# Decode attention with a gated MLP on one core: one weight load cut into three by lanes and rows, and the input loaded in one transfer

## The chip, the cores and the metric

The kernel runs on one core of one Trainium2 chip. The metric is the device time of one execution in microseconds (us). Before the change it is 661.74 us, the median of three runs (661.59, 661.74, 661.86).

The core has a tensor engine (PE), a vector engine (DVE), a scalar engine (ACT), a general engine (POOL) and a synchronization engine (SP). Transfers are started from the queues of SP and ACT, and sixteen DMA engines, shared by both queues, move the bytes.

## The reference

The result is `x + A(layernorm(x)) + B(layernorm(x))` for 4 batch entries of one token with D = 640, all in bf16. A is attention over a cache of 4096 positions, 32 heads of 128; B is a small gated MLP. Cut to what matters:

```python
def _A_ref(x, k_cache, v_cache, wq, wo):      # caches: (4, 32, 4096, 128)
    q = (x @ wq).reshape(B, Sq, Hq, Dh).transpose(0, 2, 1, 3)
    scores = jnp.einsum('bhqd,bhkd->bhqk', q, k_cache) * Dh ** (-0.5)
    p = softmax(scores, axis=-1)
    o = jnp.einsum('bhqk,bhkd->bhqd', p, v_cache)
    return o.transpose(0, 2, 1, 3).reshape(B, Sq, Hq * Dh) @ wo      # wo: (4096, 640)

def _B_ref(x, w_in, w_sp, b_sp, w_out):       # w_in: (640, 1728), w_out: (864, 640)
    z = gelu(x @ w_in)
    g = w_sp * layernorm(z[..., Fh:]) + b_sp
    return (z[..., :Fh] * g) @ w_out

xn = layernorm(x)
return x + _A_ref(xn, ...) + _B_ref(xn, ...)
```

The two caches are 134 MB each, so nearly all of the 282 MB that the kernel reads are caches. Each is read once.

## The kernel before

**Units.** The 32 heads are cut into four groups of eight. A unit `u` is one group and one batch entry, so there are sixteen. For a unit the 8 heads × 4096 positions are spread over the 128 lanes (partitions) of the on-chip memory: each lane holds 256 positions of one head, 64 KB of K and 64 KB of V. A transfer of one unit's K or V is 8 MB, 64 KB a lane.

**Scores.** DVE multiplies K by the query (`product`, L539), adds the two halves of the head dimension (`fold_half`, L545), and PE sums the rest with an identity matrix (`sums`, L557). Four such steps make a unit. DVE then reduces to scores and maxima (L571 to L590), ACT takes the exponential (L598), DVE spreads it by head (L609), and PE weights V with it (`weighted`, L633).

**Groups.** After the four units of a group, `group_turn` (L674 to L693) divides by the denominators and transposes on DVE, and `group_proj` (L701) multiplies by the group's eight rows of output weights `wo_sb`, adding into `out_ps`. The last group is done with its own layout by head.

**Places.** K goes through a ring of seven slots of 16 KB a lane; V has one place, `v_all`, which holds `wq` and `w_in` before the first V. The output weights of a group lie in ring slot 4 (`WO_AT`), 10,240 bytes a lane: 8 rows of 640 bf16. Lane `p` gets rows `8p` to `8p + 7` of the group's weights, which lie side by side in memory.

**Order of loads.** All big loads are issued on SP's queue, in the order of the list `loads`. `pump()` issues the next one as soon as the code that frees its slots stands behind it in the program; on the chip SP then waits for the semaphores of the instructions that used the slot. For a group in the middle the order is V of unit u, K of unit u + 2, and after the group's fourth V and K the group's `wo` (L235 of `load_wo`), then the next V. The small x goes on ACT's queue at the very start (L103), three transfers of 2, 1 and 1 of its four rows, into ring slot 1.

**Semaphores.** The transfers of both queues share eight completion semaphores in turn, the x loads among them: a transfer first waits for the one that had its semaphore eight transfers earlier. The first x load has semaphore 0, `wq` 1, the other two x loads 2 and 3, the first two K loads 4 and 5, the two one-element loads of the MLP (L737, L738) 6 and 7; `w_in` comes next and waits for semaphore 0, `w_out` for 1, and so on.

**B's output weights.** The 864 rows of `w_out` are three parts: 5 rows on each of 128 lanes, 1 row on each of 128 lanes, and 8 rows on each of 12 lanes; the last is loaded by four transfers (L126) of three lanes each, 10,240 bytes a lane.

Of the kernel before, what the change touches and what calls it, by code (L numbers as in the profile page):

```python
# [17 lines left out]
def kernel(  # L18
# [14 lines left out]
    nc = tc.nc  # L33
    P = nc.NUM_PARTITIONS
# [31 lines left out]
    def up(n):  # L66
        return -(-n // 256) * 256

    PW = sum(up(r * D) for _, r, _ in W_OUT[1:])
    CUT = (0, 320, D)  # L70
    CB = 4
    NG = NR // CB
    GW = CB * Dh
    QH = QD // PAR
    JR = Dh // QH
# [18 lines left out]
    p_end = p_buf[:, 2 * NR * HT :]  # L94
    p_m = p_buf[:, 0 : 2 * NR * HT].rearrange("p (n g c h) -> p n g c h", n=2, g=NG, c=CB)

# [1 line left out]

    ring = places.tile([P, RING, QW], BF16, name="k_ring")
    x_bf = ring[0:Bsz, 1, 0:D]  # L100
    x_rows = A_x.flatten_outer_dims()
    for b0, b1 in ((0, 2), (2, 3), (3, 4)):
        nc.scalar.dma_start(out=x_bf[b0:b1], in_=x_rows[b0:b1])  # L103
    v_all = places.tile([P, NK * QW], BF16, name="v_all")

    wq_sb = v_all[:, 0 : DC * HD].rearrange("p (c n) -> p c n", c=DC)
# [87 lines left out]
    def wo_load(hg):  # L194
        return (lambda: load_wo(hg)), [WO_AT]
# [27 lines left out]
    wo_sb = ring[:, WO_AT, 0 : HT * D].rearrange("p (h n) -> p h n", n=D)  # L223

    def load_wo(hg):
        rows = A_wo[hg * HT * Dh : (hg + 1) * HT * Dh]
        if hg == HG - 1:
            by_head = rows.rearrange("(h p) n -> p h n", p=P)
            for h0, h1 in ((0, 2), (2, 4), (4, 6), (6, 7)):
                nc.sync.dma_start(out=wo_sb[:, h0:h1, :], in_=by_head[:, h0:h1, :])  # L230
            for half in range(2):
                cols = slice(CUT[half], CUT[half + 1])
                nc.sync.dma_start(out=wo_sb[:, HT - 1, cols], in_=by_head[:, HT - 1, cols])
            return
        nc.sync.dma_start(  # L235
            out=wo_sb, in_=rows.rearrange("(p j) n -> p j n", j=JR)
        )

    pump()

# [4 lines left out]
    for e in range(PAR):  # L245
        nc.gpsimd.tensor_copy(
            out=of_row[:, e, :, :, e, :],
            in_=ident[:].rearrange("p (k q) -> p q k", q=QD)[:, 0:Bsz, :, None].to_broadcast(
                [P, Bsz, NQ, LN]
            ),  # L250
# [18 lines left out]
    for i in range(NSTAT):  # L269
# [5 lines left out]
        out=rstd[:], in_=mv[:, 1:2], func=ACT.Sqrt, bias=eps_tile[:Bsz], scale=1.0  # L275
# [4 lines left out]
        out=xn_bf,  # L280
# [12 lines left out]
    for c in range(DC):  # L293
        nc.tensor.transpose(
            out=xnT_ps[:, c, :], in_=xn_v[:, c, :], identity=ident[:Bsz, :Bsz]
# [8 lines left out]
    for e in range(PAR):  # L304
        q_ps = ps_pv.tile([P, HG, Dh], FP32, tag="pv", name="q_ps")
        for c in range(DC):
            for k in range(NQ):
                nc.tensor.matmul(  # L308
                    out=q_ps[k * QD : (k + 1) * QD],
# [5 lines left out]
        rows = const.tile([P, HG, Dh], BF16, name=f"q_rows{e}")  # L315
        nc.vector.tensor_scalar(  # L316
            out=rows[:], in0=q_ps[:], scalar1=scale_qk, scalar2=None, op0=ALU.mult
# [4 lines left out]

    hot = const.tile([P, CB, HT], FP32)
    nc.vector.tensor_reduce(
        out=hot[:].rearrange("p c h -> p (c h)"),
        in_=ident[:].rearrange("p (g m) -> p m g", m=QD),
        axis=AX.X,
        op=ALU.add,
    )
    pick = const.tile([P, CB, P + Bsz - 1], FP32)  # L330
    nc.gpsimd.memset(pick[:], 0.0)
    nc.gpsimd.tensor_copy(
        out=pick[:, :, Bsz - 1 :].rearrange("p c (k q) -> p c k q", q=QD)[
            :, :, :, 0 : PAR * Bsz : Bsz
        ],
        in_=hot[:].rearrange("p c (k e) -> p c k e", e=PAR),
# [4 lines left out]
        out=of_set[:],  # L341
        in_=hot[:].rearrange("p c h -> p (c h)")[:, 0 : PAR * Bsz].rearrange(
            "p (e b) -> p e b", b=Bsz
        ),
# [5 lines left out]
    with nc.allow_low_precision("0 and 1"):  # L350
        nc.vector.tensor_reduce(
            out=own[:],
            in_=ident[:].rearrange("p (h l) -> p h l", h=HT),
# [5 lines left out]
        out=par[:], in_=own[:].rearrange("p (k e) -> p e k", e=PAR), axis=AX.X, op=ALU.add  # L359
# [3 lines left out]
        out=far[:],  # L363
# [6 lines left out]

    out_ps = ps_out.tile([P, max(CUT[1], D - CUT[1])], FP32)
    OG = 32

    def out_sum(half, rows=Bsz):
        return out_ps[OG * half : OG * half + rows, 0 : CUT[half + 1] - CUT[half]]

    for half in range(2):
        nc.tensor.matmul(  # L378
            out=out_sum(half, OG),
            lhsT=ident[:Bsz, :OG],  # L380
            rhs=x_bf[:, CUT[half] : CUT[half + 1]],
            start=True,
# [19 lines left out]
    def gmlp():  # L402
# [100 lines left out]
        for k, (w, _, n, _) in enumerate(w_rows):  # L503
            for half in range(2):
                nc.tensor.matmul(
                    out=out_sum(half),
                    lhsT=gm["yT"][0:n, k, :],
                    rhs=w[:, CUT[half] : CUT[half + 1]],
                    start=False,
# [97 lines left out]
    def by_head(u):  # L607
        hg, b = divmod(u, Bsz)
        nc.vector.tensor_tensor(  # L609
            out=p_m[:, u % 2],  # L610
            in0=p_c.pop(u)[:].rearrange("p (g c) -> p g c", c=CB)[:, :, :, None].to_broadcast(
                [P, NG, CB, HT]
# [85 lines left out]
    def group_proj(hg):  # L698
        for n, o in enumerate(gr.pop(hg)):
            for half in range(2):  # L700
                nc.tensor.matmul(  # L701
                    out=out_sum(half),
                    lhsT=o,
                    rhs=wo_sb[:, n, CUT[half] : CUT[half + 1]],
                    start=False,
# [29 lines left out]
    with tc.manual_schedule(engines={E.PE, E.DVE, E.Activation, E.SP}):  # L735
# [5 lines left out]
        for n in range(NK * NU):  # L741
# [55 lines left out]
            out=den[:],  # L797
# [12 lines left out]
        for c in range(NC):  # L810
            nc.tensor.matmul(  # L811
                out=o_last[0][:, :, :, b],
# [44 lines left out]
```

## Time and profile before

| | before |
|---|---|
| median of the runs | 661.74 us |
| the profiled execution's own time | 661.84 us |
| its span in the profile | 660.0 us |
| bytes read from HBM | 282.24 MB |
| mean rate over the span | 428 GB/s |
| PE busy | 313.5 us, 47% |
| DVE busy | 522.5 us, 79% |
| ACT busy | 29.9 us, 5% |
| POOL busy | 6.4 us, 1% |
| granted clock of PE, mean | 0.68 |
| `wo` loads of groups 0 to 2, issue to landing | 20.3 us, median |

The span runs from the first to the last instruction of the profiled execution; its own time is 1.84 us more. Besides busy times the profile has the chain of work that ended last, a timeline of each engine's instructions and of the DMA issues of each queue, and records of the DMA engines: of every packet its start, its duration and its size (not which engine moved it), and of every transfer the times at which the DMA engines raised its completion semaphore.

### The profile page before, as it was taken

The numbers are of one execution on the slowest core, as the hardware profiler recorded it, in microseconds if no ns is written. First come the engines' busy times: TensorE is split into PE (matmuls) and PEld (weight loads), VectorE is DVE, ScalarE is ACT, GpSimd is POOL, SyncE is SP. The second block draws the span as 40 slices with busy tenths as digits, with TensorE's granted clock in tenths as the row PEclk, the third lists the DMA queues.
The fourth block names the chain that finished last, engine by engine and source line by source line (L and its number), as shares of the span: only waits on it lengthen the run. The fifth ranks groups of instructions, "written<-read, shape, count | busy, mean of one in ns | idle before, by whom it ended". The sixth has DMA issues, their size and how long they took to land.

```text
span 660.0 us, 4780 instructions
## 1 busy us (share of the span) xinstructions
PE 313.5 (47%) x2083; PEld 134.3 (20%) x2083; DVE 522.5 (79%) x274; ACT 29.9 (5%) x73; POOL 6.4 (1%) x21
## 2 busy tenths in 40 slices
PE   0564362536426362462536436363462634637366
PEld 0231120212212121130212212121130211212124
DVE  1767978969597795969959598695969969999960
ACT  0020000000000000000000000000000000000000
POOL 2100000000000000000000000000000000000000
PEclk9665585766858677675865767667676866776566
DMA  9999999999999999999999999999999999999997
GB/s 372 434 454 441 413 441 438 425 441 442 421 441 434 433 434 433 433 418 437 442 441 437 410 441 441 434 429 429 434 441 433 434 417 449 413 435 434 449 408 289
DMA packets 8224, 282.55 MB, mean 428 GB/s; under 512 B 888, under 2 KB 2176, under 8 KB 2560
## 3 DMA queue, kind: packets, MB, share of 16 engines
q1 hardware_dynamic: 8184, 282.24, 99.1%
q8 instruction: 16, 0.26, 0.1%
q14 instruction: 4, 0.03, 0.0%
q10 hardware_dynamic: 20, 0.01, 0.0%
HBM read 282.24 MB, written 0.01 MB: 428 GB/s over the span
## 4 chain that ended last, share of the span: by engine, by line
DMA 62%; DVE 28%; PE 9%; issue 1%; ACT 0%; DVEq 0%
DMA k_ring<-in_A_k_cache_dram 53%; DVE k_ring L539 14%; DVE k_ring L545 7%; PE s_ps L557 6%; DMA v_all<-in_A_v_cache_dram 4%; DMA k_ring<-in_A_wo_dram 3%; DVE s_sb L571 3%; DMA v_all<-in_A_wq_dram 2%; DVE p_m L609 1%; DVE m L580 1%; PE pv L633 1%; PE out_ps L701 1%; DVE p_m L680 1%; PE q_ps L308 1%; DVE mf L582 1%
## 5 line engine op out<-in xcount | busy, mean ns | idle before, releaser
L557 PE MATMUL s_ps<-k_ring,ident 128*128 128x512 bf16 x512 | 203.2, 569 | 318.0 <-DVE k_ring L545 317.9
L539 DVE TENSOR_TENSOR k_ring<-k_ring,qbc 128x8192 bf16<-128x8192 bf16 x64 | 282.9, 4420 | 89.2 <-DMA k_ring<-in_A_k_cache_dram 88.6
L557 PEld LDWEIGHTS <-ident 128*128 128x128 bf16 x512 | 64.2, 131 | 434.8 <-issue 245.6
L545 DVE TENSOR_TENSOR k_ring<-k_ring 128x4096 bf16<-128x4096 bf16 x64 | 145.9, 2280 | 1.1
L633 PE MATMUL pv<-v_all,p_m 128*32 128x512 bf16 x960 | 61.4, 413 | 0.0
L571 DVE TENSOR_REDUCE s_sb<-s_ps 128x128 f32<-128x1024 f32 x32 | 39.0, 1218 | 3.7 <-PE s_ps L557 3.7
L609 DVE TENSOR_TENSOR p_m<-p_c,own 128x2048 bf16<-128x2048 bf16 x16 | 36.6, 2285 | 0.7 <-ACT p_c L598 0.7
L633 PEld LDWEIGHTS <-p_m 128*32 128x32 bf16 x992 | 26.6, 105 | 41.2 <-issue 21.5
L598 ACT ACTIVATE p_c<-s_sb,nm 128x256 bf16<-128x256 f32 x16 | 8.1, 509 | 344.4 <-DVE nm L590 344.4
L664 PEld LDWEIGHTS o_ps<-o_rows,pick 128*128 128x128 f32 x96 | 19.1, 276 | 4.0 <-issue 3.1
L664 PE MATMUL o_ps<-o_rows,pick 128*128 128x128 f32 x96 | 18.0, 350 | 0.0
L645 ACT COPY o_rows<-pv 128x512 f32<-128x512 f32 x16 | 9.4, 586 | 163.2 <-PE pv L633 163.1
L819 DVE TENSOR_TENSOR o_n_last<-o_last,rden_all 128x32 bf16<-128x32 f32 x1 | 0.2, 193 | 12.2 <-PE o_last L811 12.2
L270 DVE BATCH_NORM_STATS2 stats<-k_ring 4x6 f32<-4x320 bf16 x2 | 0.9, 473 | 10.8 <-DMA k_ring<-in_A_x_dram 10.8
L529 ACT CAST qbc<-qbc_ps 128x128 bf16<-128x128 f32 x16 | 4.3, 266 | 91.2 <-PE qbc_ps L521 91.2
L580 DVE TENSOR_REDUCE m<-s_sb 128x1 f32<-128x256 f32 x16 | 6.7, 420 | 0.5
L521 PE MATMUL qbc_ps<-q_rows,of_row 128*128 128x128 bf16 x32 | 6.3, 289 | 0.6 <-DVE q_rows L316 0.6
L521 PEld LDWEIGHTS <-of_row 128*128 128x128 bf16 x32 | 4.4, 140 | 8.1 <-issue 7.8
L378 PE MATMUL out_ps<-k_ring,ident 4*32 4x320 bf16 x2 | 0.4, 429 | 10.8 <-DMA k_ring<-in_A_x_dram 10.8
L701 PE MATMUL out_ps<-k_ring,p_m 128*4 128x320 bf16 x48 | 4.7, 350 | 1.8 <-DVE p_m L693 1.8
L316 DVE TENSOR_SCALAR q_rows<-q_ps 128x512 bf16<-128x512 f32 x2 | 1.4, 692 | 4.4 <-PE q_ps L308 4.4
L409 PE MATMUL zT<-xnT,v_all 128*12 128x4 bf16 (+1 forms) x140 | 4.7, 170 | 0.0
(86 smaller groups left out, 81.5 us busy)
## 6 DMA issues: line engine op xcount, KB each, us to landing
k_ring<-in_A_k_cache_dram SPq DMA_DIRECT2D x5, 4096.0 KB
v_all<-in_A_v_cache_dram SPq DMA_DIRECT2D x2, 4096.0 KB, 29.3
v_all<-in_A_wq_dram SPq DMA_DIRECT2D x1, 5120.0 KB, 15.4
k_ring<-in_A_k_cache_dram SPq DMA_DIRECT2D x2, 2048.0 KB
k_ring<-in_A_v_cache_dram SPq DMA_DIRECT2D x1, 4096.0 KB
k_ring<-in_A_wo_dram SPq DMA_DIRECT2D x3, 1280.0 KB, 20.3
v_all<-in_B_w_in_dram SPq DMA_DIRECT2D x1, 2160.0 KB
k_ring<-in_A_v_cache_dram SPq DMA_DIRECT2D x1, 2048.0 KB
```

What stands on the lines that cost most here:

```text
L521: nc.tensor.matmul(out=qb_ps[:], lhsT=of_row[:, e, b].rearrange("p k f l -> p (k f l)"), rhs=q_rows[e][:, hg, :], start=(e == 0), stop=(e ...
L539: nc.vector.tensor_tensor(out=t, in0=t, in1=qbcs[u][:, None, :].to_broadcast([P, HC, Dh]), op=ALU.mult)
L545: nc.vector.tensor_tensor(out=t[:, :, 0:HD2], in0=t[:, :, 0:HD2], in1=t[:, :, HD2:Dh], op=ALU.add)
L557: nc.tensor.matmul(out=s, lhsT=ident[:], rhs=t[:, :, g * RW : (g + 1) * RW], start=(g == 0), stop=(g == m - 1),)
L571: nc.vector.tensor_reduce(out=scores[u][:].rearrange("p (r c) -> p r c", r=NK)[:, lo : hi + 1 : hi - lo], in_=sums_ps.pop(n // 2)[:], axis ...
L580: nc.vector.tensor_reduce(out=m1[:], in_=scores[u][:], axis=AX.X, op=ALU.max)
L598: nc.scalar.activation(out=p_c[u][:], in_=scores.pop(u)[:], func=ACT.Exp, bias=maxes.pop(u)[:], scale=1.0, accum_out=row_den[hg % NACC][:, ...
L609: nc.vector.tensor_tensor(out=p_m[:, u % 2], in0=p_c.pop(u)[:].rearrange("p (g c) -> p g c", c=CB)[:, :, :, None].to_broadcast([P, NG, CB, HT]
L633: nc.tensor.matmul(out=pvs[u][cg * QD : (cg + 1) * QD, :], lhsT=p_m[:, u % 2, g0 + n].rearrange("p c h -> p (c h)"), rhs=v_at[:, n * CB : ...
L645: nc.scalar.copy(out=o[:].rearrange("p c d -> p (c d)"), in_=pvs.pop(u)[:])
L664: nc.tensor.matmul(out=gr[hg][:], lhsT=pick[:, c, Bsz - 1 - b : P + Bsz - 1 - b], rhs=o[:, c, :], start=(b == 0 and c == 0), stop=(b == Bs ...
L701: nc.tensor.matmul(out=out_sum(half), lhsT=o, rhs=wo_sb[:, n, CUT[half] : CUT[half + 1]], start=False, stop=(hg == HG - 1 and n == HT - 1),)
```

## The change

Two edits, and the line numbers that follow from them:

```diff
     CUT = (0, 320, D)
+    LOW = 115
     CB = 4
...
     x_bf = ring[0:Bsz, 1, 0:D]
-    x_rows = A_x.flatten_outer_dims()
-    for b0, b1 in ((0, 2), (2, 3), (3, 4)):
-        nc.scalar.dma_start(out=x_bf[b0:b1], in_=x_rows[b0:b1])
+    nc.scalar.dma_start(out=x_bf, in_=A_x.flatten_outer_dims())
...
-        nc.sync.dma_start(
-            out=wo_sb, in_=rows.rearrange("(p j) n -> p j n", j=JR)
-        )
+        by_lane = rows.rearrange("(p j) n -> p j n", j=JR)
+        if hg != 1:
+            nc.sync.dma_start(out=wo_sb, in_=by_lane)
+            return
+        for l0, l1 in ((0, LOW), (LOW, P)):
+            nc.sync.dma_start(out=wo_sb[l0:l1, 0, :], in_=by_lane[l0:l1, 0, :])
+        nc.sync.dma_start(out=wo_sb[:, 1:JR, :], in_=by_lane[:, 1:JR, :])
```

For group 1 alone the one transfer of 128 lanes × 8 rows becomes three: the first row of lanes 0 to 114, the first row of lanes 115 to 127, and the other seven rows of all lanes. The bytes and their places stay the same. The four rows of x are loaded by one transfer.

In the built program the instructions of PE, DVE and POOL stand in the same order as before. ACT issues two transfers less at the start, and SP two more at group 1. Because the eight semaphores are taken in turn, every transfer between the start and group 1's weights has a semaphore two places further on than its old one would be; after group 1's weights the places are the old ones. At the start `w_in` and `w_out` no longer wait for a semaphore, the 1-row part of `w_out` waits for x, the third K load for `wq`, and the four transfers of the 12-lane part for the first two K loads and the two one-element loads. The K load after group 1's weights waits for the semaphores of all three pieces.

## The prediction

> **What bounds the kernel now.** I read the page's DMA part first, then the chain of work that ended last, then the timeline of SP's queue, and last the records of single packets.
>
> ```profile
> span 660.0 us, 4780 instructions
> DMA  9999999999999999999999999999999999999997
> DMA packets 8224, 282.55 MB, mean 428 GB/s; under 512 B 888, under 2 KB 2176, under 8 KB 2560
> q1 hardware_dynamic: 8184, 282.24, 99.1%
> q8 instruction: 16, 0.26, 0.1%
> ```
>
> The DMA engines are busy from the first slice to the last, and SP's own transfers (q1) fill 99.1% of them. The kernel is a stream of bytes; compute matters only where it holds back an issue so long that an engine runs dry.
>
> ```profile
> 0.73 15.39 DMA v_all<-in_A_wq_dram
> 16.13 0.04 issue
> 16.17 3.81 PE q_ps L308 x40
> ...
> 349.25 27.27 DMA k_ring<-in_A_k_cache_dram
> ...
> 389.78 1.94 PE out_ps L701 x16
> 391.74 26.41 DMA k_ring<-in_A_k_cache_dram
> ...
> 633.99 21.98 DMA k_ring<-in_A_wo_dram
> 655.97 0.04 issue
> 656.01 1.31 PE out_ps L701 x8
> ```
>
> In the chain (start, us, what), compute starts on `wq`'s landing at 16.13, not on x; the kernel ends on the last group's weights. Their last half row lands at 656.84 by its semaphore records; PE ends 0.48 later, then come the copy and the store.
>
> ```profile
> 349.25 0.33 SPq L166 DMA_DIRECT2D k_ring<-in_A_k_cache_dram  x1
> 358.18 0.33 SPq L235 DMA_DIRECT2D k_ring<-in_A_wo_dram  x1
> 363.03 0.33 SPq L177 DMA_DIRECT2D v_all<-in_A_v_cache_dram  x1
> 391.74 0.33 SPq L166 DMA_DIRECT2D k_ring<-in_A_k_cache_dram  x1
> ```
>
> SP is always a transfer ahead (timeline: start, us, issue): V is issued at 363.03 and K's first engine ends only at 373.25 (`wo` behind it at 376.31); the K of 391.74 comes 3.9 us before V's first engine ends at 395.62. The tightest such place later is V at 608.71, 2.7 us before the first engine is through the K ahead of it (611.37). A first packet follows its issue by 1.0 us (0.73 to 1.74 for `wq`), so no engine runs dry.
>
> So there are sixteen independent streams, and the time is that of the latest. By the semaphore records of the last half row they end, in us against the last one:
>
> ```
> -3.27 -3.00 -2.75 -2.12 -1.81 -1.44 -1.39 -1.32 | -0.57 -0.43 -0.39 -0.32 -0.30 -0.26 -0.20 0.00
> ```
>
> Why two halves? Each packet starts 3 to 4 ns before the end of its predecessor, so packets can be strung into sixteen chains. The sixteen 16 KB instruction packets (q8) fall on eight chains, twice on each; one takes about 0.95 us and lengthens a data packet beside it by about 0.5. Those eight are the late half. The other eight have none. Three of them carry the four extra 10,240-byte rows of the 12-lane part (1.55 us); they are -1.81, -1.44 and -1.32. I call an engine by the share that it takes of a transfer: those three are engines 0 to 2.
>
> **The change, part by part.** From start to start, a 1,280-byte packet costs 52 ns, 8,192 bytes 306, 10,240 bytes 381, the 4-byte semaphore packet 6 (medians over the chains). Between the middle two, 8,960 bytes (seven rows) are 334 by straight line, my estimate.
>
> *Shares.* The records count how many engines raise a semaphore: 2 for a transfer of 2 lanes, 3 for 3, 4 for the 4-lane store, 16 for 128, always the same number of lanes each. The even split of 115 onto at most sixteen is 5 × 23, that of 13 is 13 × 1. I take that, with shares on the lowest engines, as the chain of the 1-lane transfers is one of the three of the 3-lane ones. No transfer of 115 lanes is in the trace, so other splits are rivals. The Trainium skill states this rule (DMA: Bandwidth & Descriptors, section on why a DMA increments its semaphore by 16): the largest divisor up to 16, on the lowest-numbered engines; the counts of 2, 3, 4 and 16 agree.
>
> *Work moved.* Every engine loses 8 × 381 and gains 8 × 334: -0.375 us. Engines 0 to 4 gain 24 rows at 52 ns and two semaphore packets: +1.260, net +0.885. Engines 5 to 12 gain one row and one semaphore packet: +0.058, net -0.317. Engines 13 to 15: -0.375.
>
> *Where it lies.* The streams never run dry, so each shift lasts to the end. Engines 0 to 2 stand at -1.32 or earlier and go to -0.435 or earlier. The eight late chains go down by 0.317 or 0.375. Are engines 3 and 4 early? Eight chains take instructions and 0 to 2 are not among them; five of the other thirteen are early. If the eight are one block of neighbours at the top, 3 and 4 are early. I take that; the other case is a rival. Then the latest is a late chain at -0.32 to -0.37; I take -0.33.
>
> *SP's queue.* Two more issues at 0.43 us each (the duration of back-to-back issues near 16.5 us) stand before V: 0.86 us inside the 4.85 us in which V waits anyway; without that cover they would still be hidden in the ten until 373.25. The K of 391.74 now waits for three pieces; `wo` landed at 379.55, so the pieces land near 380.5 and `group_proj` needs them at 389.78.
>
> *x.* One transfer of four 1,280-byte rows, one on each of engines 0 to 3, for three. The 2-row piece landed at 2.03, the single rows at 7.62 and 10.70, because each went to engine 0 behind `wq` packets of 1.51 us. Now x should be there near 2.1 and layer norm, 10.82 to 14.99, moves forward by 8.7 us. It is worth nothing: PE waits for `wq` until 16.13. Nor does it cost, unless x landed after 12.0. Engine 0 loses two rows (-0.10), engines 2 and 3 gain one (+0.06); all are taken as early chains.
>
> *Waits at the start.* `w_out` is issued near 3 us instead of 16.15, with `wq`, two K pieces and `w_in` ahead of it in the same queue either way (`w_in` lands at 31.00). The third K load still waits for `wq`, the 12-lane part for landings at 20.96 to 26.26 as before. Nothing.
>
> Sum: 660.0 - 0.33 = 659.7 of span, 661.5 with the 1.84 around it (own time 661.84). The profiled run lay 0.10 above the median, so 661.74 - 0.33 = 661.4.
>
> **Rivals.**
>
> *The lanes are shared, not the engines (slower).* In before every engine of a 128-lane load keeps its own eight lanes. The 115-lane row lets five engines write into lanes that others are filling. If that shares a way into the memory, both run at half rate there: a row costs 104 ns, engines 0 to 4 gain 24 × 0.104 + 0.012 - 0.375 = +2.13, and the latest of 0 to 2 ends at +0.81: 662.5. It decides from 1.685 / 24 = 70 ns a row (1.32 + 0.375 - 0.012 = 1.683). For it: sixteen engines at 65,536 bytes in 2.414 us are 434 GB/s, and no slice holds much more. Against: the late half is late through its instruction packets, so a way that is held up by an engine has room. The longest 1,280-byte packet of the trace, 152 ns, bounds this at 24 × 0.148 + 0.012 - 0.375 - 1.32 = +1.9, 663.6; the other bound is the 52 ns used. The Trainium skill speaks for this rival (the same page, section on where 436 GB/s comes from): the ports of the on-chip memory are the bottleneck, not the engines. The 434 agree; no run here tells port from engine.
>
> *Engine 3 or 4 is a late one.* Then one of -0.57 to 0.00 gets +0.885: +0.3 to +0.9, 662.0 to 662.6.
>
> *No effect: the rows are dealt out unevenly, eight to an engine.* Then most engines get eight single rows and one of the 13: -0.375 + 9 × 0.052 + 0.012 = +0.1: 661.8.
>
> *All 115 rows on one engine.* 115 × 0.052 - 0.375 + 0.064 = +5.67 on engine 0, less its lead of 1.44: +4.2, 665.9 to 666.0. Against: every multi-lane transfer of the trace is split.
>
> *Faster by more.* The mean of the sixteen ends is -1.22 us: no dealing of the same bytes can win more than 1.2: 660.5, under 0.2%.
>
> **How the numbers follow.** Measurement tells about 0.2% from no change, 1.3 us here. Forecast 0.55 (661.2 to 661.6); shared lanes 0.17; a late engine 0.10; no effect 0.08; one engine 0.04; unnamed 0.06, half of it over the bound on the slow side, a third on the fast. Over 0.2% slower are the one-engine case, a fifth of the shared lanes and half the unnamed: 0.10. Faster: 0.02. The rest, 0.88, is within. The range takes the forecast and the first three rivals without their worst: 660.9 to 662.6.
>
> **What would show it.** In after: the last transfer's sixteen ends drawn together, from 3.27 us to about 3; the 115-lane piece raised by five engines; its packets 52 ns apart (over 70: shared lanes); x landing near 2 and layer norm starting there, with PE's L308 still at 16.2; V still issued well before 373. Wrong would be an end of the last half row not earlier than 656.84, or one chain alone behind.

## The result, and the profile after

| | before | after |
|---|---|---|
| median of the runs, measured side by side (22 each) | 661.75 us | 662.42 us |
| lowest to highest | 661.58 to 662.08 | 662.21 to 664.41 |
| span of the profiled execution | 660.0 us | 660.9 us |
| bytes read from HBM | 282.24 MB | 282.24 MB |

The change costs 0.67 us by the medians. The ratio is 1.0013, with a 95% interval of 1.0007 to 1.0019 (1.0010 by the medians alone). The forecast was -0.33 us. Two of the 22 runs (664.26 and 664.41) lie some 2 us above the rest, as do 7 of the 33 runs of four experiments below that cut the lanes too (by 2 us or more) and none of any other kernel, for a reason that stays open: the medians hardly feel them, the ratios do.

The page of after, its head and the DMA part:

```profile
span 660.9 us, 4781 instructions
...
DMA  9999999999999999999999999999999999999997
...
DMA packets 8370, 282.55 MB, mean 428 GB/s; under 512 B 906, under 2 KB 2322, under 8 KB 2706
...
q1 hardware_dynamic: 8330, 282.24, 99.2%
```

The same bytes go in 146 more packets, and SP's queue still fills the engines. The chain of work that ended last, of after (start, us, what):

```profile
0.73 15.48 DMA v_all<-in_A_wq_dram
16.21 0.04 issue
16.26 4.40 PE q_ps L311 x40
...
32.38 30.60 DMA k_ring<-in_A_k_cache_dram
63.00 4.42 DVE k_ring L542
...
349.20 28.42 DMA k_ring<-in_A_k_cache_dram
...
390.88 2.03 PE out_ps L704 x15
392.93 26.21 DMA k_ring<-in_A_k_cache_dram
...
634.76 22.13 DMA k_ring<-in_A_wo_dram
656.89 0.04 issue
656.93 1.27 PE out_ps L704 x8
```

Read it against the chain of before. The K transfer issued at 349.2 has one piece of 28.42 us where it had 27.27. That is K of the fourth unit of group 1, which lies just ahead of the changed weights in the streams, and it has landed 1.10 us later than it did. `group_proj` (now L704) follows 1.10 us later, and the next K is issued at 392.93, not 391.74. The end on the last weights is 0.92 us later. At the start `wq` lands 0.08 us later, and PE's 40 matmuls behind it take 4.40 us for 3.81. The K that is issued next goes out 0.68 us later for it, but DVE starts on it at 63.00 as in before, so that was worth nothing. The two lines of before:

```profile
31.70 31.27 DMA k_ring<-in_A_k_cache_dram
63.00 4.43 DVE k_ring L539
```

SP's issues around the changed load (timeline of SP, start, us, issue):

```profile
349.20 0.33 SPq L165 DMA_DIRECT2D k_ring<-in_A_k_cache_dram  x1
358.14 0.66 SPq L239 DMA_DIRECT2D k_ring<-in_A_wo_dram  x2
358.85 0.35 SPq L240 DMA_DIRECT2D k_ring<-in_A_wo_dram  x1
361.95 0.35 SPq L176 DMA_DIRECT2D v_all<-in_A_v_cache_dram  x1
```

All three pieces are in the queue by 359.2, and V at 361.95 is even 1.1 us earlier than before. No DMA engine waited for an issue here. So the engines had work throughout; did they do less of it? The table of stretches says so. Its columns are the stretch, its length, the busy time of PE, PE's weight loads, DVE, ACT and POOL (with counts), PE's granted clock, the DMA engines' busy share, and GB/s. First before, then after:

```profile
330.00:360.00 30.00, 13.51 (x56) 5.86 (x59) 23.00 (x13) 0.87 (x3) 0.00 (x0) 0.56 1.00 433
360.00:390.00 30.00, 14.12 (x88) 6.40 (x82) 21.93 (x17) 1.45 (x4) 0.00 (x0) 0.67 1.02 440
390.00:420.00 30.00, 16.25 (x112) 7.03 (x108) 22.41 (x8) 0.59 (x1) 0.00 (x0) 0.73 0.99 428
```

```profile
330.00:360.00 30.00, 14.17 (x68) 6.62 (x71) 23.05 (x13) 0.87 (x3) 0.00 (x0) 0.58 0.98 426
360.00:390.00 30.00, 11.62 (x70) 5.00 (x62) 20.86 (x13) 1.19 (x3) 0.00 (x0) 0.70 1.02 424
390.00:420.00 30.00, 17.02 (x115) 7.20 (x113) 22.44 (x11) 0.85 (x2) 0.00 (x0) 0.73 1.01 435
```

Look at the last two columns of the middle row. The share is 1.02 in both, yet the rate falls from 440 to 424 GB/s. (A packet is counted where it starts, so single stretches scatter by some per cent, in the share and in the rate alike; a fall of the rate at an unchanged share is what counts.) The engines were busy, but their packets took longer.

The records of single packets say which. In before, from 10 us on, a packet of one size takes nearly the same time everywhere, but for those beside an instruction packet. In after one stretch stands out, 371.8 to 377.8 us, in which they do not. Packets that start between 365 and 390 us and took over 20 ns more than the shortest of their size:

```
size, B   packets   shortest   median   longest    lengthened   by, in all
 1,280      128        55 ns     64 ns    114 ns        26         0.8 us
 8,960      128       338       395.5     580           86         9.1
65,536      138      2418      2418      3458           15         4.9
```

Together 14.8 us. 0.5 us of it is a K packet beside an instruction packet, as in before; the other 14.3 us are 0.89 us for each of sixteen streams. (That 0.5 is left out of the sums of this kind below.) The single rows are lengthened little. What is slowed are the large packets of the *other* transfers beside them: K's, and the seven-row piece's.

The semaphore records show the same shift, in us of the first and the last engine:

```
                       before             after
K ahead of it      373.25 to 376.52   373.46 to 377.62
group 1's weights  376.31 to 379.55   377.41 to 380.53
last half row      653.57 to 656.84   654.48 to 657.71
```

And the ends of the last half row of after, against its last:

```
-3.23 -3.14 -2.33 -1.69 | -0.85 -0.67 -0.67 -0.64 -0.61 -0.57 -0.51 -0.44 -0.34 -0.28 -0.10 0.00
```

Twelve streams now end within 0.85 us, where eight ended within 0.57. That is what the shares as worked out would do. But all streams are later.

### The profile page after: what moved, and what is told of

Its sections match the earlier page's. It is cut to its first block, busy times and chain, and to the rows that moved or that the text cites. A ratio compares the mean times of both kernels' runs of the same rounds, so it can differ in the third digit from the quotient of the medians.

```text
span 660.9 us, 4781 instructions
## 1 busy us (share of the span) xinstructions
PE 315.7 (48%) x2083; PEld 135.8 (21%) x2083; DVE 522.5 (79%) x274; ACT 29.7 (4%) x73; POOL 10.2 (2%) x21
## 3 DMA queue, kind: packets, MB, share of 16 engines
q1 hardware_dynamic: 8330, 282.24, 99.2%
HBM read 282.24 MB, written 0.01 MB: 427 GB/s over the span
## 4 chain that ended last, share of the span: by engine, by line
DMA 62%; DVE 28%; PE 9%; issue 1%; DVEq 0%; ACT 0%
DMA k_ring<-in_A_k_cache_dram 53%; DVE k_ring L542 14%; DVE k_ring L548 7%; PE s_ps L560 6%; DMA v_all<-in_A_v_cache_dram 4%; DMA k_ring<-in_A_wo_dram 3%; DVE s_sb L574 3%; DMA v_all<-in_A_wq_dram 2%; DVE p_m L612 1%; DVE m L583 1%; PE out_ps L704 1%; PE q_ps L311 1%; DVE p_m L683 1%; PE pv L636 1%; DVE mf L585 1%
## 5 line engine op out<-in xcount | busy, mean ns | idle before, releaser
L311 PE MATMUL q_ps<-v_all,xnT 128*32 128x512 bf16 x40 | 4.4, 620 | 9.9 <-DMA v_all<-in_A_wq_dram 9.9
L704 PE MATMUL out_ps<-k_ring,p_m 128*4 128x320 bf16 x48 | 5.7, 403 | 1.8 <-DVE p_m L696 1.8
L721 PE MATMUL o_last<-hot,o_rows 128*128 128x8 f32 x32 | 4.9, 279 | 0.7 <-ACT o_rows L648 0.7
L721 PEld LDWEIGHTS o_last<-hot,o_rows 128*128 128x128 f32 x32 | 4.8, 226 | 1.8 <-ACT o_rows L648 1.6
```

Source lines behind the costliest of these rows:

```text
L311: nc.tensor.matmul(out=q_ps[k * QD : (k + 1) * QD], lhsT=xnT[:, c, :], rhs=wq_v[:, c, k, e], start=(c == 0), stop=(c == DC - 1),)
L704: nc.tensor.matmul(out=out_sum(half), lhsT=o, rhs=wo_sb[:, n, CUT[half] : CUT[half + 1]], start=False, stop=(hg == HG - 1 and n == HT - 1),)
L721: nc.tensor.matmul(out=o_last[0][:, :, :, u % Bsz], lhsT=o[:, c, :], rhs=hot[:, c, :].rearrange("p (k e) -> p k e", e=PAR), start=(c == 0) ...
```

## The experiments

The theory after the result, A: a row that is written by another DMA engine than the one that has its lane in the 128-lane loads holds up that engine's packets. In a 128-lane load each of sixteen engines has eight lanes, so the five engines of the 115-lane piece can own at most 40 of its rows: at least 75 rows of after are such rows. The rivals: B, the pattern in which single rows 10,240 bytes apart are read from memory; besides, the uneven shares of the engines, and x with the semaphores. Diffs are against the changed kernel where nothing else is said.

**x alone** (the weights' load as before).

> Only x in one transfer; the group's weights as before. Theory A (the single rows are written into lanes that other DMA engines are filling, and both slow down there) and theory B (the single rows are slow to read, because they are cut out of rows that are read at the same time) both expect no effect: 661.65 to 661.85, since the first matrix product still waits for wq. A rival, that the moved transfer times at the start carry part of the loss, expects 661.95 or more.

Measured 661.77 us, before 661.77; ratio 1.0001 (0.9992 to 1.0009). x costs nothing and brings nothing. Why it brings nothing can be read in the groups of the first 17 us (line, engine, operation, names, shapes, count, busy us, mean ns, idle before and its releaser). Before, then after:

```profile
L308 PE MATMUL q_ps<-v_all,xnT 128*32 128x512 bf16 x9 | 1.4, 620 | 1.5 <-DMA v_all<-in_A_wq_dram 1.5
...
L270 DVE BATCH_NORM_STATS2 stats<-k_ring 4x6 f32<-4x320 bf16 x2 | 0.9, 473 | 10.8 <-DMA k_ring<-in_A_x_dram 10.8
```

```profile
L311 PE MATMUL q_ps<-v_all,xnT 128*32 128x512 bf16 x8 | 1.0, 616 | 9.9 <-DMA v_all<-in_A_wq_dram 9.9
...
L273 DVE BATCH_NORM_STATS2 stats<-k_ring 4x6 f32<-4x320 bf16 x2 | 0.9, 474 | 2.5 <-DMA k_ring<-in_A_x_dram 2.5
```

DVE waits for x 8.3 us less, and PE waits for `wq` 8.4 us more (PE waits for `wq` 10.0 us in the run with x alone). In after x landed at 2.52 instead of 10.70, and a wait for `wq` took its place.

**The three-part load alone** (x in three transfers again).

```diff
-    nc.scalar.dma_start(out=x_bf, in_=A_x.flatten_outer_dims())
+    x_rows = A_x.flatten_outer_dims()
+    for b0, b1 in ((0, 2), (2, 3), (3, 4)):
+        nc.scalar.dma_start(out=x_bf[b0:b1], in_=x_rows[b0:b1])
```

> Only the three-part load of the second group's weights; x in three transfers as before. Theories A and B: the whole loss of the change, 662.3 to 662.6. If x carried part of the loss: 662.2 or less.

Measured 662.48, before 661.77; ratio 1.0021 (1.0013 to 1.0030). By the medians +0.71, the whole effect: x and the order of the semaphores at the start have no part in it. Four of its twelve runs took 664.35 to 664.95; they raise the ratio.

**Row 0 on all lanes in one transfer.**

```diff
-        for l0, l1 in ((0, LOW), (LOW, P)):
+        for l0, l1 in ((0, P),):
```

> x in one transfer; the first row on all 128 lanes in one transfer, then the seven rows: sixteen engines with eight 1,280-byte rows each. Same packets and the same source as in the changed kernel. Theory A: each engine stays with its own lanes, no packet is lengthened (8,960 bytes take 338 ns), each engine pays -0.375 + 8 x 0.052 + 0.006 = +0.05 us: 661.75 to 661.9. Theory B: the seven-row packets are lengthened as in the changed kernel (median near 395 ns), 662.2 or more.

Measured 661.85, before 661.77; ratio 1.0001 (0.9993 to 1.0010). All 8,960-byte packets took 338 ns and all single rows 55. The same 128 rows are read from the same places and written to the same places as in after; what differs is the engine that carries each, and that one transfer moves them instead of two. The row of its table that answers to those above:

```profile
360.00:390.00 30.00, 12.39 (x80) 5.85 (x70) 21.54 (x16) 1.45 (x4) 0.00 (x0) 0.72 1.02 440
```

440 GB/s again, as before.

**Row 0 cut at 112 lanes.**

```diff
-    LOW = 115
+    LOW = 112
```

> x in one transfer; the first row cut at lane 112 instead of 115, so that 112 and 16 lanes split evenly over sixteen engines: every engine has eight single rows, as with one transfer of 128 lanes, but engine e gets lanes 7e to 7e + 6, if shares are runs of lanes, which in the transfers of 128 lanes belong to another engine for most lanes. Theory A: packets are lengthened as in the changed kernel: 662.3 to 662.9, without the uneven shares. Theory B: the same as with the first row in one transfer, whatever that is. No lengthened packet at all in both would leave the five-engine shares as the cause.

112 and 16 lanes are 7 and 1 rows for each of sixteen engines: the shares are those of the kernel with one transfer, so uneven shares are out of it. Measured 662.35, before 661.77; ratio 1.0009 (1.0000 to 1.0018). The 8,960-byte packets had a median of 365 ns and a longest of 538, 72 of them lengthened by 5.7 us in all; with the others 8.7 us, 0.54 a stream. The shares add 0.05, and the medians are 0.58 apart. The table has the fall of the rate again, at a share of 1.01:

```profile
360.00:390.00 30.00, 12.95 (x78) 5.84 (x70) 21.00 (x14) 1.23 (x4) 0.00 (x0) 0.66 1.01 427
```

This and the last run differ in the engine of each row and in one transfer more (one 4-byte semaphore packet more for each engine). Even shares do not help: the loss does not need the uneven shares of after, nor its five busy engines.

**The source pattern: rows side by side.** Both kernels take the single rows from rows that lie side by side in memory instead of 10,240 bytes apart; the projection of group 1 then uses other rows than the reference. First with 115 and 13 lanes, then with 128.

```diff
-            nc.sync.dma_start(out=wo_sb[l0:l1, 0, :], in_=by_lane[l0:l1, 0, :])
+            nc.sync.dma_start(out=wo_sb[l0:l1, 0, :], in_=rows[l0:l1])
```

> As the changed kernel (115 and 13 lanes, five and thirteen engines, the same places in the on-chip memory), but the single rows are read from 128 rows that lie side by side instead of every eighth row; the second group's weights of the first row of each lane are thereby other rows. Theory A (the lanes written to): packets lengthened as before, 8,960 bytes at a median near 390 ns, 662.2 to 662.6. Theory B (cut out of rows that are read at the same time): no lengthening, 661.4 to 661.6.

> As the kernel with the first row on 128 lanes in one transfer, read from the 128 rows that lie side by side; the second group's weights of the first row of each lane are thereby other rows. Which engine reads which place in HBM changes, which engine writes which lane does not. Theory A: no lengthened packet, 661.75 to 661.9. If it is the pairing of engine and source that costs: lengthened packets, 662.2 or more.

Measured against 661.64 before: 662.38 with 115 and 13 (1.0014, 1.0005 to 1.0023), 661.78 with 128 (1.0002, 0.9993 to 1.0011). With 115 and 13 the 8,960-byte packets had a median of 411.5 ns; with 128 none was lengthened. B fell: reading the rows from other places, with the same writes, made no difference; cutting the lanes does.

**Row 0 in two halves** (`LOW = 64`).

> x in one transfer; the first row cut at lane 64: two transfers of 64 lanes, sixteen engines with four single rows each, eight rows in all, the same even shares as with 112 and 16 lanes. If shares are runs of lanes, about half of the 128 rows are written into lanes of another engine, against 113 of 128 with the cut at 112. Theory A: about half of that lengthening (9.9 us over all engines there): 662.0 to 662.2. A theory that any cut costs as much: 662.3 to 662.4.

Measured 662.49, before 661.64; ratio 1.0013 (1.0004 to 1.0022). The lengthening was 10.4 us between 370 and 380 us, and 0.05 + 10.4/16 = 0.70, against the 0.85 between the medians. But I had expected half of the 112-lane kernel's loss and got more than all of it. My count of the rows that two halves give to other engines is wrong, or the loss does not go with that count alone. The traces do not tell which engine moved which row, so this stays open.

**B's output weights on the early engines instead.** An attempt to unload the late engines without crossing lanes; everything else as in the kernel before.

```diff
-    W_OUT = ((P, 5, 1), (P, 1, 1), (12, 8, 4))
+    W_OUT = ((P, 5, 1), (32, 7, 4))
```

> The kernel before, with other shares of B's output weights: five rows on 128 lanes as before, and the other 224 rows as seven on each of lanes 0 to 31, by four transfers of eight lanes four apart, in place of one row on 128 lanes and eight on 12 lanes. Same result. Each of eight engines then writes lanes 4e to 4e + 3, which are its own if lanes are dealt in fours. Theory A: no lengthened packet; the late engines lose 8 x 0.052 + 0.006 = 0.42 us, engines 3 to 7 gain 0.94, engines 0 to 2 lose 0.6; the last stream ends 0.42 earlier: 661.3 to 661.5, faster than before. If work can't be moved between engines at all without loss: 661.75 or more.

Each of the four transfers takes every fourth of 32 lanes, one lane an engine, as the 12-lane part does. Measured 662.53, before 661.64; ratio 1.0014 (1.0005 to 1.0022). All 32 packets of 8,960 bytes, the moved rows, took 338 ns, and from 10 us on the lengthening over the whole kernel was 11.0 us, against 9.7 in before. So a few lanes can be loaded by few engines without lengthened packets. It is slower for another reason, which the ends of the last half row show:

```
-3.61 -3.12 -2.98 -2.94 -2.88 -2.73 -2.54 -2.46 -1.71 -1.41 -1.37 -1.36 -1.35 -1.25 -0.20 0.00
```

Two streams stand alone, 1.05 us or more behind the rest. They must be two of engines 0 to 7, which got four packets more, and late ones: two of the eight that fetch instructions. The other late ones end at 657.59 - 1.25 = 656.34, 0.50 earlier than before. My expectation had taken the eight late engines for the upper block, as the prediction had.

**How the loss grows: all eight rows cut at 112 lanes, and three groups.** The first has two transfers of 10,240 bytes a lane and no third; the second has after's load, cut at 112, in all of groups 0 to 2.

```diff
-            nc.sync.dma_start(out=wo_sb[l0:l1, 0, :], in_=by_lane[l0:l1, 0, :])
-        nc.sync.dma_start(out=wo_sb[:, 1:JR, :], in_=by_lane[:, 1:JR, :])
+            nc.sync.dma_start(out=wo_sb[l0:l1], in_=by_lane[l0:l1])
```

```diff
-        if hg != 1:
-            nc.sync.dma_start(out=wo_sb, in_=by_lane)
-            return
```

> All eight rows of group 1's weights on 112 lanes and on 16 lanes, in two transfers (x in one). Every engine moves eight packets of 10,240 B as before, so the shares are the old ones (one semaphore packet more, +0.01 us). With the single row cut at 112 (e4) 112 packets of 1,280 B, 5.8 us of engine time at 52 ns, lengthened the others by 9.3 us in all, 0.58 us a stream. Theory that the loss goes with the bytes written by engines that do not have the lanes: 112 packets of 10,240 B at 381 ns are 42.7 us, 7.3 times as much; 0.58 x 7.3 = +4.3 us, about 666 (665 to 667), and the lengthened packets now include the 10,240 B ones. Rival, that it goes with the number of packets: +0.6, about 662.3. Rival, that it comes of a single-row transfer running beside the seven-row one (two transfers with one destination): none here, 661.7 to 661.9.

> The load in three pieces, cut at 112 lanes as in e4, for the groups 0, 1 and 2 instead of 1 alone (x in one transfer). Theory that each such load costs every stream some 0.6 us for good, since no stream ever catches up: three times the +0.58 of e4, +1.75, about 663.4 (662.9 to 664.0), with lengthened packets in three stretches, near 180, 375 and 570 us. Rival, that the streams have slack somewhere and the loss is in part made good, or that e4's excess is chance: 662.0 to 662.6.

All eight rows: 666.28 against 661.78, ratio 1.0075 (1.0059 to 1.0090), +4.50 us by the medians where bytes gave +4.3 and the number of packets +0.6. Every engine moves the bytes and packet sizes of before, and one 4-byte semaphore packet more; what has changed is who writes which lane. Two transfers alone do not explain it: the row on all lanes, followed by the other seven, was two transfers too, and cost nothing. The rate falls furthest here, at a busy share of 1.00:

```profile
360.00:390.00 30.00, 9.46 (x67) 4.47 (x60) 18.36 (x10) 1.19 (x3) 0.00 (x0) 0.71 1.00 352
```

The 128 packets of 10,240 bytes had a median of 769 ns (385 in before) and 43 packets of 65,536 bytes took up to 5122 ns (2418): 50.9 + 37.1 = 88.0 us with the 0.5 beside an instruction packet, 5.5 a stream. (That profiled execution took 668.45 us, 2.2 above the median, and one of its streams alone ended 1.45 us behind all the others.)

Three groups: 664.02 against 661.78, ratio 1.0047 (1.0024 to 1.0069). The medians are 2.24 apart (one of the six runs took 668.4); the lengthened packets lie in three stretches, by 6.5 us from 210, 8.6 from 370 and 9.2 from 530 (10 us each), 24.3/16 = 1.52 a stream, and the shares add 0.16. The losses add up: none is made good later. The measured value lies just above what was expected (664.0).

**Does the lengthening account for the loss?** The median goes by the latest stream alone. A closer account is the mean of the sixteen ends of the last half row in each profiled execution. Beside it stand a sixteenth of the lengthening and what the shares add to the mean, all in us against before:

```
                            lengthening   shares   mean of the ends   last end
after                          0.89        0.05         +1.09          +0.87
x alone                        0           0            -0.03          -0.17
three-part load alone          0.80        0.05         +0.89          +0.54
row 0 on all lanes             0           0.05         +0.07          -0.01
row 0 cut at 112               0.54        0.05         +0.69          +0.56
side by side, 115 and 13       0.78        0.05         +0.89          +0.62
side by side, 128              0           0.05         +0.04          -0.15
row 0 in two halves            0.65        0.05         +0.78          +0.86
B's output weights             0          -0.03         -0.02          +0.75
all eight rows at 112          5.48        0.01         +5.71          +6.70
three groups at 112            1.52        0.16         +1.85          +1.80
```

Lengthening and shares together come within 0.25 us of the mean in every row. The last end differs from the mean because losses and shares fall unevenly on the streams. With B's output weights the streams lost nothing in the mean; the work lies on the wrong ones.

None of the kernels was faster than the kernel before.

## Why the prediction was wrong

*Right: what bounds the kernel.* The end is that of the latest of sixteen streams that never run dry. Lengthening and shares account for the mean of the sixteen ends to within 0.25 us in every kernel of the table above.

*Right: the shares.* The 115-lane piece was raised by five engines and the 13-lane one by thirteen. That is 5 × 23 and 13 × 1, if each engine has as many as the next. The even, the uneven-by-eight and the one-engine dealings are out. No stream stands alone behind the others in after, so engines 3 and 4 were early ones, and that rival fell too. That the late eight are one block at the top was wrong (two lie among engines 5 to 7), but cost nothing here, since every engine from 5 up lost 0.317 or more.

*Right: the sizes in themselves.* 8,960-byte packets that nothing disturbs took 338 ns by the record, 334 from start to start as estimated.

*Right: all that was costed at nothing.* V was issued 11.5 us before the first engine had finished the K ahead; layer norm moved forward behind PE's wait for `wq`; x alone gave 661.77 for 661.77. The K of 391.74 went out 1.19 us later because its data and the projection came later, not because it had three semaphores to wait for.

*Wrong: the price of crossing lanes.* The step that failed is "Engines 0 to 4 gain 24 rows at 52 ns" and its companion for 5 to 12, with nothing for what these rows do to others. The late eight were to go down by 0.317 to 0.375. They did lose that work, and a stream got 0.89 us of lengthening in return on average: -0.32 + 0.89 = +0.57, where the medians rose by 0.67 and the last end of the profiled execution by 0.87. That 662.42 lies within the range is owed to the rivals, not to the forecast's working. The first rival named the likely place, lanes that others are filling, and its 662.5 is close to the time. But that closeness is luck, for its mechanism is half wrong: it put the loss on the rows, 104 ns each on engines 0 to 4, and made it decide from 70 ns. The rows had a median of 64. The loss fell on the large packets beside them, 13.5 of 14.3 us, and so on the late streams too. My argument against it, that the way of a late engine has room because instruction packets hold that engine up, did not hold: the late streams ended later as well, and away from the instruction packets the 65,536-byte packets of before take 2415 to about 2418 ns throughout, so a late engine's are no faster and no slower than another's.

*What is shown, and what is not.* Shown: with source, destination, sizes and shares held the same, cutting the 128 lanes into 112 and 16 costs, and the cost grows with the bytes (1 row against 8). The number of transfers, the shares and the places read are out, so what is left is which engine writes which lane; no record names the engine of a row. Not shown: whether it is the foreign lane as such that costs, or that more engines than usual write into one part of the lanes at once; and what it is that the lanes share. That the loss is some two times the crossing rows' own time is an estimate: 112 × 0.381 us doubled is 85 us, against 88.0; 112 × 0.052 doubled is 11.6, against 8.7. The two halves do not follow it: by their expectation only half of the 128 rows cross, 64 × 0.052 doubled is 6.7, and 10.4 was measured. The estimate would fit a way into each set of lanes that one engine alone already fills, so that a crossing packet costs its own time and the owner's.

The Trainium skill describes such a way (SBUF — State Buffer, section on the DMA port swizzle): sixteen ports, each serving eight lanes in two runs of four. The Trainium skill says further (DMA: Bandwidth & Descriptors, section on the descriptor swizzle) that in a 128-lane transfer each engine has the eight lanes of one port. The four transfers over 32 lanes that would give each engine, by that page, only a lane of its own run of four, and lengthened none of the moved packets, agree with it; which lanes share a port, no run here shows.

## What to carry to other kernels

Where a stream of 128-lane transfers keeps all DMA engines full, a transfer over another number of lanes, or one cut into runs of lanes, need not be free even if it moves the same bytes with perfectly even shares: one row of 1,280 bytes a lane, cut at 112 lanes, cost 0.6 us for good here, and eight such rows 4.5. When you rebalance such engines, try first a way that should leave each lane to its engine (the one tried here lengthened no moved packet), and look for the price in the packets of the *other* transfers: a busy share that stays while GB/s falls. And before adding work to "the early engines", identify the late ones by measurement: two of them sat where I had not looked.

## What was not expected of the hardware

- Most of the lost time is that of the large packets beside the small ones that cross: 13.5 of 14.3 us, though by the median both take about a sixth longer (8,960 bytes 395.5 ns for 338, 1,280 bytes 64 for 55). With both sides large (10,240 beside 65,536) both go to twice their time and above: 769 for 385, up to 5122 for 2418.
- One row on 112 of 128 lanes, written with even shares, cost nearly as much as the 115-lane one whose shares were uneven: +0.58 against +0.67 and +0.71. Two runs of 64 lanes cost +0.85. Part of that may be where the loss fell, since the mean of the ends rose by 0.78 only, less than after's 1.09; that it is more than with the cut at 112 I can't explain.
- Instruction fetches fall on eight of the sixteen engines, and not on the upper eight: two are among engines 5 to 7, by the ends of the run with B's output weights.
